# The first batch's a and b by column halves, a later place for the second weight halves, and wider, longer-lasting warm-up products

## The chip, the cores and the metric

The kernel runs on one core of one Trainium2 chip. The metric is the device time of one execution in microseconds (us); the median of several runs counts. A core has a matrix engine (TensorE, PE in the profile), VectorE (DVE), ScalarE (ACT), GpSimd (POOL) and SyncE (SP), which here does nothing but issue the DMAs.

## The reference

Attention with a decay bias, then two feed-forward stages, all float32. There are 4 batches, 8 heads, 576 positions, 64 values per head, and so 2304 tokens of 512 values.

```python
scores = q @ k.T / 8 + minimum(-(cum_i - cum_j), 0)    # masked above the diagonal
attn   = exp(scores - max);  attn /= attn.sum() + 1e-9
x = (attn @ v)                       # tokens x 512, heads side by side
a, b = x @ w1, x @ w2                # 512 -> 1024 each
h = (a * b) @ w3;  x2 = h @ w_out    # -> 1024 -> 512
h2 = x2 @ w_in                       # -> 2048
out = (h2 - tanh(h2)) @ w_out2       # -> 512
```

## The kernel before

All matrix operands after the first heads are split into a rounded high part and a low part (names ending in h and l: `xh`, `xl`, `w1h`, `w1l`, ...), and each product is three matmuls: high by high, low by high, high by low.

Nothing is issued directly. Every operation is handed to a planner (`Plan`) with its duration by a table, the buffers that it reads and writes, a priority (smaller is earlier), and, for copies and subtractions, a choice of engines. `Plan.order` lets model time run and gives each free engine the ready operation of least priority; the order that comes out is the order in which the instructions stand on each engine. On the chip each engine works through its list in that order, so an instruction that waits holds up all that stand behind it on its engine.

The start of the kernel, with which the change deals:

- **Heads.** `head` does one head: scores for tiles of queries into two PSUM banks (L568, or L570 and L571 in the split form), a DVE reduction that adds the mask, copies the scores out and takes the row maximum (L579, one for each score bank), `exp` on ACT (L585), transposes on PE (L615), the copy of their result out of PSUM on ACT (`eh`) with the low part by DVE (`el`, L322), and the product with the values (L650 in float32; L652 and L655 in the split form), whose result DVE adds up into `xf` (L662). Two heads' buffers (`e0`, `e1`, `rqk0`, `rqk1`) are in turn. Group 0 of a head is queries 0 to 319, group 1 queries 320 to 575. For batch 0 all eight heads do group 0 first, then all eight do group 1 (only the first two of this second pass in float32); batch 1 is likewise done by groups. The normalized result is split into `xh`, `xl`.
- **Weights.** `convert` loads 128 x 512 numbers of float64 (`wraw`, 512 KB), makes float32 of them with one ACT operation (L422) and four of DVE (L423, L424, L426, L428, into one of three `wt` buffers), and splits that into high (ACT or DVE) and low (POOL or DVE, L324 or L322). `w1` and `w2` are 16 such pieces: 8 for columns 0 to 511 (priority 790), 8 for columns 512 to 1023 (the second halves, priority 790 + `convq`).
- **a and b.** `products(b, half)` does, for one half of a batch's queries (288), the eight column blocks f = 0 to 7 of a and b: 12 matmuls of 288 columns each for a and for b (L710), so 24 for a block, and then a copy `asb` and a DVE product into `cst` (L718). Blocks 0 to 3 need the first weight halves only, blocks 4 to 7 the second. Their PE priority is above 1.0e6, behind every head's. The next batch's heads go on while PE works at them.
- **Warm-up products.** `filler` is a bf16 matmul on zeros. One stands at the start; and wherever PE would be idle in model time before `fu`, `Plan.order` puts as many as fit. Before the change that ends with the first matmul of `products`.

The rest of the kernel (from some 400 us) computes `wa` = w3 by w_out, x2, and the last stage; the change does not touch it.

Of the kernel before, what the change touches and what calls it, by code (L numbers as in the profile page):

```python
# [34 lines left out]
XT = [(t, min(t + 512, NT)) for t in range(0, NT, 512)]  # L35
MASKED8 = -8.0e9
NR = D + 10
PARAM = dict(dsub=1000.0, dsub0=1000.0, dcopy=1000.0, dcopy0=600.0, dother=1000.0, dother0=1000.0, spi=500.0, lay=6, lay0=4, layp=2.2e5, layf=2.95e5, gate=0, dve0=1000.0, early=100.0e3, raw0=0, rawp=-700.0, ng=3, nosb=2, cut=(1,), convq=400.0, natb=2, abk=1, wap=0.95e6, dve=1000.0, act=0.0, pool=0.0, sem=160.0, pesem=180.0, slow=1.1, convp=790.0, npre=4,
             nbias=3, keep=0.5, ff=0.0, fu=60.0e3, wlast=8, bw=370.0, ntr=3, actb=1, actn=0, spp=-80.0, ne=2, nsb=2, ncf=5, outlag=15)

LO_CLAMP = 2.0 ** -15 * 1.125
HI_CLAMP = 2.0 ** 16 * (2.0 - 2.0 ** -3 - 2.0 ** -20)
# [18 lines left out]


class Op:
    __slots__ = ("opts", "eng", "lat", "fn", "prio", "deps", "succ", "n", "ready", "start", "end", "dur", "as_", "ae", "two", "kind")


class Plan:
# [14 lines left out]
    def op(self, opts, r=(), w=(), prio=0.0, lat=0.0, two=False, kind=None):  # L82
        o = Op()
        o.kind = kind
        o.two = two
        o.opts = {e: (d, fn) for e, d, fn in opts}
        o.prio, o.lat, o.eng = prio, lat, None
        o.deps = set()
# [21 lines left out]
    filler = None  # L110

    def busy(self, a, b):
        while a < b:
# [13 lines left out]
    def order(self):  # L127
# [30 lines left out]
                push(o)  # L158
        done = []
        pair = 0.0  # L160
        while True:
            best = None
            for e in free:
# [31 lines left out]
                free[e] = t + 50.0  # L195
                continue
            if e == "PE":
                if got.prio >= 1.0e6:
                    self.fill_until = 0.0
                while self.fill_from < free[e] and free[e] + 60.0 < t < self.fill_until:  # L200
                    f = Op()
                    f.eng, f.fn, f.start, f.prio, f.lat, f.deps = e, self.filler, free[e], 9e9, 0.0, ()
                    f.dur = 60.0 * self.clock(free[e])
                    f.end = f.start + f.dur
                    self.busy(f.start, f.end)
                    done.append(f)
                    free[e] = f.end
                t = max(t, free[e])
            got.eng = e
            got.dur, got.fn = got.opts[e]  # L210
            if e == "POOL" or (e == "DVE" and got.two):
                t = max(t, pair)
# [4 lines left out]
            if e == "PE":  # L217
                self.busy(t, got.end)
            free[e] = got.end
            done.append(got)  # L220
            for x in got.succ:
                x.n -= 1
# [35 lines left out]
def tile_kernel(ctx, tc, qk, v, s, w1, w2, w3t, w_out, w_in, w_out2, out):  # L258
# [51 lines left out]
    wt_d = Buf(NF2)  # L310
    wt_d.t = dram.tile([NF2, P, 512], F32, name="wt_d")


    def dma(dst, src, nbytes, r, w, prio):
        pl.op([("SP", max(PARAM["spi"], 60.0 + nbytes / PARAM["bw"]), lambda: nc.sync.dma_start(dst(), src()))], r=r, w=w, prio=prio, lat=2000.0)
# [18 lines left out]
    def dve(fn, n, r, w, prio, fast=False, two=False, extra=0.0):  # L334
        pl.op([("DVE", c_dve(n, fast) + extra, fn)], r=r, w=w, prio=prio, two=two or fast)
# [10 lines left out]
    wu = keep.buf("wu", [P, 32])  # L346
# [12 lines left out]
    asb_r = abp.ring("asb", 2, [P, HALF])  # L359

    att = Pool("att", "right")
    msk = att.buf("msk", [P, S])
# [91 lines left out]
    def values():  # L454
        m = nc.vector.memset
        m(fix.t[:NH], 1.0)
        m(fix.t[D:D + 5], 1.0)
        for R in rqk:
            m(R.t[D:D + 32, S:], 0.0)
        m(const.t[:, 0:1], SQ_B)  # L460
        m(const.t[:, 1:2], -T2)
        m(ssum.t, 1.0)
        m(msk.t, 0.0)
# [7 lines left out]
    pl.op([("DVE", 2700.0, values)], w=[const, ssum, msk, eh, el, en, fix] + [(R, 1) for R in rqk] + e2, prio=-2900)  # L471
# [6 lines left out]
    pl.op([("POOL", 3000.0, patterns)], w=[ident, (fix, 1), msk], prio=-2500)  # L478


    def constants(i):
# [4 lines left out]
    dve(lambda: nc.vector.memset(wu.t, 0.0), 32, [], [wu], -3000, fast=True)  # L486
# [5 lines left out]
    pe(50.0, filler, [wu], [bank[7]], -3000)  # L492

    for i in range(2):
        dma(lambda i=i: rqk[i].t[D:D + 5, :S], lambda: fix.t[D:D + 5], 5 * S * 4, [(fix, 1)], [(rqk[i], 1)], -990)
# [195 lines left out]
            split(lambda: XH.t[:, c, qa:qb], (XH, ps), lambda: XL.t[:, c, qa:qb], (XL, ps), lambda: X.t[:, qa:qb], qb - qa, [X], pr + 110)  # L691


    def products(b, half):
        XH, XL = xh[b % 2], xl[b % 2]
        o = half * HALF
        for f in range(NF):
            if f % 2 == 0:
                cs = cst_r.next()
            ab = []  # L700
            for wh, wl in ((w1h, w1l), (w2h, w2l)):
                bk = ab_ring.next()

                for k0 in range(0, KC, PARAM["abk"]):
                    ks = range(k0, min(k0 + PARAM["abk"], KC))

                    def mm(bk=bk, wh=wh, wl=wl, f=f, ks=ks):
                        for k in ks:
                            for j, (w_, x_) in enumerate(((wh, XH), (wh, XL), (wl, XH))):
                                nc.tensor.matmul(bk.t[:, :HALF], w_.t[:, k, f * P:(f + 1) * P], x_.t[:, k, o:o + HALF],  # L710
                                                 start=k == 0 and j == 0, stop=k == KC - 1 and j == 2)
                    parts = [k * 2 + f // 4 for k in ks]
                    xs = [2 * k + g for k in ks for g in range(1 + half)]
                    pe(3 * len(ks) * c_pe(HALF), mm, [(XH, xs), (XL, xs), (wh, parts), (wl, parts)], [bk], 1.0e6 + ((b * 2 + half) * NF + f))
# [27 lines left out]
    for b in range(B):  # L742
# [7 lines left out]
        else:  # L750
# [175 lines left out]
```

## Time and profile before

| | before |
|---|---|
| runs | 996.61, 997.66, 1001.73 us; median 997.66 |
| the profiled execution | 1001.11 us, of which the span from first to last instruction is 999.3 us |
| PE, DVE, ACT, POOL busy | 97%, 72%, 60%, 39% of the span |
| TensorE's mean granted clock | 0.976 of full |

A share of busy time is a mean over stages. The "granted clock" is the share of TensorE's full rate that the chip let through: 1.00 is 2.4 GHz, 0.50 is 1.2 GHz. PE's busy time is modelled, and at half clock everything on it takes about twice as long, so a busy PE may do half the work; the number of matmuls in a stretch (x..) says more. The trace may lack a few matmul records.

### The profile page before, as it was taken

To read this page: it belongs to the slowest core of one execution; us is meant where nothing else is said; L and a number is where in the kernel's file an instruction comes from. 1 tells how busy PE (TensorE), PEld (TensorE's weight loads), DVE (VectorE), ACT (ScalarE), POOL (GpSimd) and SP (SyncE) were. 2 spreads that over 40 slices of the span, in tenths; PEclk is the share of its full clock that TensorE was granted. 3 is DMA by queue.
4 is the path that set the end of the run, shared out by engine and by line. 5 is a ranking of instruction groups with operands and counts; after the bars stand their busy time and mean duration, and the time that the engine had idled before them with its cause. 6 is when DMAs were issued, how large, how long until landed. Compare 5 with 4: busy or idle time off the path is not lost.

```text
span 999.3 us, 16720 instructions
## 1 busy us (share of the span) xinstructions
PE 967.4 (97%) x5715; PEld 839.3 (84%) x5715; DVE 720.6 (72%) x1453; ACT 602.8 (60%) x1378; POOL 393.8 (39%) x338
## 2 busy tenths in 40 slices
PE   7988799999998999999999999999999999999998
PEld 6557599999998999888988898878888888888897
DVE  7579878887898876998688879895544545545455
ACT  4575577878887874444354538566545555555565
POOL 2245646643654633433254647442222222222221
PEclk7799699999999999999999999999999999999999
DMA  5476246565555413546769865103002100200010
GB/s 160 134 210 204 91 123 191 179 193 176 159 158 153 131 48 110 183 166 231 248 234 334 275 216 201 42 22 127 1 1 85 43 0 1 85 1 1 1 43 22
DMA packets 70093, 124.47 MB, mean 125 GB/s; under 512 B 6780, under 2 KB 39172, under 8 KB 70008
## 3 DMA queue, kind: packets, MB, share of 16 engines
q1 hardware_dynamic: 70008, 123.41, 38.7%
q8 instruction: 45, 0.74, 0.3%
q14 instruction: 40, 0.33, 0.1%
HBM read 93.34 MB, written 25.99 MB: 119 GB/s over the span
## 4 chain that ended last, share of the span: by engine, by line
PE 85%; DVE 6%; DMA 3%; issue 2%; ACT 2%; POOL 1%; SPq 0%; DVEq 0%; ACTq 0%; POOLq 0%
PE bank L851 19%; PE bank L710 16%; PE bank L874 6%; PE bank L873 6%; PE bank L872 6%; PE bank L615 5%; PE bank L815 3%; PE bank L814 3%; PE bank L813 3%; PE bank L570 2%; PE bank L652 2%; PE bank L655 2%; PE bank L571 2%; PE bank L568 2%; PE bank L775 1%
## 5 line engine op out<-in xcount | busy, mean ns | idle before, releaser
L324 POOL TENSOR_TENSOR gl<-pg,gh 128x512 fp32r<-128x512 f32 (+1 forms) x78 | 98.6, 1264 | 261.0 <-ACT gh L318 248.0
L851 PE MATMUL bank<-x2b,wih 128*128 128x512 f32 (+1 forms) x640 | 183.0, 371 | 0.0
L862 DVE TENSOR_TENSOR pg<-bank,u 128x512 f32<-128x512 f32 (+1 forms) x80 | 50.8, 635 | 142.7 <-ACT th L861 140.6
L851 PEld LDWEIGHTS bank<-x2b,wih 128*128 128x128 f32 x640 | 116.6, 188 | 22.5
L851 PE MATMUL bank<-x2b,wil 128*128 128x512 f32 (+1 forms) x320 | 118.7, 371 | 0.0
L874 PE MATMUL bank<-voh,gl 128*128 128x512 f32 x288 | 112.8, 392 | 0.5 <-POOL gl L324 0.4
L872 PE MATMUL bank<-voh,gh 128*128 128x512 f32 x288 | 112.7, 391 | 0.2 <-ACT gh L318 0.2
L873 PE MATMUL bank<-vol,gh 128*128 128x512 f32 x288 | 112.8, 392 | 0.0
L318 ACT ACTIVATE gh<-pg 128x512 fp32r<-128x512 f32 (+1 forms) x80 | 47.1, 589 | 87.3 <-DVE pg L866 86.6
L585 ACT ACTIVATE e<-e,nmx 64x64 f32<-64x64 f32 (+4 forms) x160 | 88.7, 556 | 12.0 <-DVE nmx L579 11.5
L615 PE MATMUL bank<-ident,e 128*128 128x128 f32 (+1 forms) x480 | 82.8, 283 | 5.1 <-DVE el L322 3.1
L859 ACT ACTIVATE u<-bank 128x512 f32<-128x512 f32 (+1 forms) x80 | 44.3, 553 | 70.9 <-PE bank L851 67.0
L422 ACT ACTIVATE wt<-wraw 128x512 f32<-128x512 f32 x72 | 47.9, 671 | 63.9 <-DMA wraw<-w3t 14.6
L710 PE MATMUL bank<-xh,w1h 128*128 128x288 f32 x256 | 81.8, 319 | 3.7 <-ACT asb L318 2.1
L579 DVE CUSTOM_DVE_ANT_0 e<-bank,msk 64x64 f32<-64x64 f32 (+4 forms) x160 | 64.5, 417 | 27.9 <-PE bank L568 14.4
L710 PE MATMUL bank<-xh,w2h 128*128 128x288 f32 x256 | 81.1, 317 | 2.9 <-DVE cst L718 2.4
L710 PE MATMUL bank<-xh,w2l 128*128 128x288 f32 x256 | 76.2, 298 | 3.0 <-POOL w2l L324 3.0
L710 PE MATMUL bank<-xh,w1l 128*128 128x288 f32 x256 | 76.6, 299 | 2.1 <-POOL w1l L324 2.1
L322 DVE TENSOR_TENSOR el<-bank,eh 128x512 fp32r<-128x512 f32 (+1 forms) x162 | 73.2, 473 | 5.0 <-ACT eh L318 4.3
L710 PE MATMUL bank<-xl,w1h 128*128 128x288 f32 x256 | 76.0, 297 | 0.0
L710 PE MATMUL bank<-xl,w2h 128*128 128x288 f32 x256 | 75.7, 296 | 0.0
L866 DVE COPY_PREDICATED pg<-mk,th 128x512 f32<-128x512 uint32 (+1 forms) x80 | 62.8, 785 | 12.5 <-ACT mk L864 4.6
(137 smaller groups left out, 2624.5 us busy)
## 6 DMA issues: line engine op xcount, KB each, us to landing
rqk<-qk SPq DMA_DIRECT2D x30, 576.0 KB
wraw<-w_out SPq DMA_DIRECT2D x24, 512.0 KB
c_d<-cst SPq DMA_DIRECT2D x32, 288.0 KB
wraw<-w SPq DMA_DIRECT2D x16, 512.0 KB
wraw<-w3t SPq DMA_DIRECT2D x16, 512.0 KB
cf<-c_d SPq DMA_DIRECT2D x32, 256.0 KB
wraw<-w_in SPq DMA_DIRECT2D x16, 512.0 KB
x_d<-x2s SPq DMA_DIRECT2D x16, 512.0 KB
```

Source lines behind the costliest of these rows:

```text
L322: o = [("DVE", c_dve(n), lambda: nc.vector.tensor_tensor(dst(), a(), b().bitcast(F32), op=ALU.subtract))]
L324: o.append(("POOL", c_pool2(n), lambda: nc.gpsimd.tensor_tensor(dst(), a(), b().bitcast(F32), op=ALU.subtract)))
L579: nc.vector.tensor_tensor_reduce(e.t[:nq, EOFF[t] + k0:EOFF[t] + k1], bk.t[:nq, :k1 - k0], bi.t[:nq, bo + k0:bo + k1], -0.125, 3.0e38 if f ...
L585: act(lambda: nc.scalar.activation(et(), et(), AF.Exp, bias=nmx.t[:nq, i, tm:tm + 1], scale=-1.0, accum_out=ssum.t[:nq, pj, t, i:i + 1]), ...
L615: nc.tensor.transpose(bk.t[:rows, n * P:(n + 1) * P], e.t[:, EOFF[t] + c * P:EOFF[t] + c * P + rows], ident.t)
L710: nc.tensor.matmul(bk.t[:, :HALF], w_.t[:, k, f * P:(f + 1) * P], x_.t[:, k, o:o + HALF], start=k == 0 and j == 0, stop=k == KC - 1 and j ...
L851: nc.tensor.matmul(bk.t[:, :w], w_.t[:, k, a], X2.t[:, i, k, :w], start=k == 0 and n == 0, stop=k == KC - 1 and n == 2)
L862: dve(lambda u=u, pg=pg, hp=hp, c_=c_: nc.vector.tensor_tensor(c_(pg), hp(), c_(u), op=ALU.mult), w, [bk, u], [pg], pr)
L866: dve(lambda pg=pg, mk=mk, th=th, c_=c_: nc.vector.copy_predicated(c_(pg), c_(mk).bitcast(U32), c_(th)), w, [mk, th], [pg], pr, two=True)
L872: nc.tensor.matmul(bank[n].t, gh.t[:, a], voh[f].t, start=f == 0, stop=False)
L873: nc.tensor.matmul(bank[n].t, gh.t[:, a], vol[f].t, start=False, stop=False)
L874: nc.tensor.matmul(bank[n].t, gl.t[:, a], voh[f].t, start=False, stop=f == NF2 - 1)
```

## The change

Four edits. `products` takes the blocks that it is to do; for batch 0 the order is blocks 0 to 3 for both halves of the queries, then blocks 4 to 7 for both, and the priorities count up in that order. `convq` goes from 400 to 1200: the second weight halves' conversions have priority 1990 in place of 1190, which is behind all heads of batch 0 (priorities up to some 1600) and among those of batch 1. The warm-up product is 128 x 128 in place of 64 x 64, reads zeros in the first 64 columns of the mask `msk`, and writes bank 2, the bank of the product with the values, in place of bank 7. And it may be put into PE's idle time up to 150 us of model time (60 before), also behind the first matmul of `products`, but not between a write and the last read of bank 2.

```diff
-... convq=400.0 ... fu=60.0e3 ...
+... byf=(0,) ... convq=1200.0 ... fu=150.0e3 ...
...
-                if got.prio >= 1.0e6:
-                    self.fill_until = 0.0
-                while self.fill_from < free[e] and free[e] + 60.0 < t < self.fill_until:
+                while self.fill_from < free[e] and free[e] + 110.0 < t < self.fill_until and not unread and free[e] >= read:
...
-                    f.dur = 60.0 * self.clock(free[e])
+                    f.dur = 107.0 * self.clock(free[e])
...
     def filler():
-        x = wu.t.bitcast(BF16)
-        nc.tensor.matmul(bank[7].t[:D, :D], x[:, :D], x[:, :D], start=True, stop=True)
+        x = msk.t[:, :D].bitcast(BF16)
+        nc.tensor.matmul(bank[2].t[:, :P], x, x, start=True, stop=True)
...
-    def products(b, half):
+    def products(b, half, fs):
...
-        for f in range(NF):
+        for f in fs:
+            pos = 1.0e6 + n_prod[0]
+            n_prod[0] += 1
...
-        for half in range(2):
-            products(b, half)
+        for fs in (range(4), range(4, NF)) if b in PARAM["byf"] else (range(NF),):
+            for half in range(2):
+                products(b, half, fs)
```

What this does to the lists of instructions is seen at three places. All lines of the changed kernel are 9 to 13 higher, and buffers have other numbers behind the underscore.

On DVE the two lists are the same up to the sum `xf1` of the third head in batch 0's second pass (the fourth head's three reductions on `e1` are done by then). Before, the conversions of the second weight halves follow it:

```order
160 L662 TENSOR_TENSOR xf1_126<-bank2_60,pvt_124 64x256
161 L428 SCALAR_TENSOR_TENSOR wt0_83<-wraw1_82,wt0_83 128x512
162 L718 TENSOR_TENSOR cst1_132<-bank7_65,asb0_133 128x288
...
170 L424 TENSOR_SCALAR wt2_89<-wt2_89 128x512
171 L423 TENSOR_SCALAR wt0_83<-wt0_83 128x512
172 L426 SCALAR_TENSOR_TENSOR wt2_89<-wraw2_88,wt2_89 128x512
173 L322 TENSOR_TENSOR el_123<-bank5_63,eh_122 64x128
174 L423 TENSOR_SCALAR wt1_84<-wt1_84 128x512
175 L424 TENSOR_SCALAR wt0_83<-wt0_83 128x512
176 L428 SCALAR_TENSOR_TENSOR wt2_89<-wraw2_88,wt2_89 128x512
```

The fifth head's first reduction comes 31 rows behind `xf1`. In the changed kernel it is the next row, and the sixth head's follow:

```order
160 L671 TENSOR_TENSOR xf1_125<-bank2_60,pvt_123 64x256
161 L588 ISA e0_115,nmx_117<-bank0_58,msk_103 128x448
162 L588 ISA nmx_117 128x1
163 L731 TENSOR_TENSOR cst1_131<-bank7_65,asb0_132 128x288
164 L332 TENSOR_TENSOR el_122<-bank3_61,eh_121 128x4x128
165 L588 ISA e0_115,nmx_117<-bank1_59,msk_103 128x288
...
173 L437 SCALAR_TENSOR_TENSOR wt0_82<-wraw1_81,wt0_82 128x512
174 L731 TENSOR_TENSOR cst1_131<-bank7_65,asb1_133 128x288
175 L332 TENSOR_TENSOR el_122<-bank5_63,eh_121 64x128
176 L588 ISA e1_116,nmx_117<-bank1_59,msk_103 128x448
```

The seven pieces of the second weight halves that are unfinished at that row (one lacks only its last operation) have moved from one block into the gaps of the next eight heads; the last of the 16 conversions stands, as before, ahead of the sum for batch 1's fourth head.

On PE, in the seventh head of that second pass, the products that stood between the heads' matmuls are gone, and warm-up products (`msk`) stand there. Before (`xh`, `xl` by w1, w2 are the products):

```order
843 L570 MATMUL bank_59<-kh_112,qs_111 128x288
844 L571 MATMUL bank_59<-kl_113,q_114 128x288
845 L710 MATMUL bank_64<-xh_90,w1h 128x288
846 L710 MATMUL bank_64<-xl_92,w1h 128x288
847 L710 MATMUL bank_64<-xh_90,w1l 128x288
848 L570 MATMUL bank_58<-kh_112,qs_111 128x288
849 L571 MATMUL bank_58<-kl_113,q_114 128x288
850 L710 MATMUL bank_65<-xh_90,w2h 128x288
```

And of the changed kernel:

```order
594 L579 MATMUL bank_58<-kh_111,qs_110 128x448
595 L580 MATMUL bank_58<-kl_112,q_113 128x448
596 L579 MATMUL bank_59<-kh_111,qs_110 128x288
597 L580 MATMUL bank_59<-kl_112,q_113 128x288
598 L499 LDWEIGHTS msk
599 L499 MATMUL bank_60<-msk 128x128
600 L499 LDWEIGHTS msk
601 L499 MATMUL bank_60<-msk 128x128
```

Counted in the two lists, there stand ahead of the eighth head's product with the values in that pass 201 matmuls of `products` before and 114 now, ahead of that of batch 1's fourth head in its first group 261 and 180, of batch 1's ninth such product 375 and 342, and from the 34th behind batch 0 on (786 ahead) the two are level again. Warm-up products: 283 before, 179 of them at the start; 218 now, 100 at the start, 47 up to the first matmul of `products`, and 71 behind it.

On SP's queue only the last three loads of the second weight halves change place among the heads' loads; before, two of them stood together:

```order
97 L315 DMA wraw3_108<-w1 128x1024
98 L315 DMA wraw2_88<-w2 128x1024
99 L315 DMA rv1_109<-v 128x320
100 L315 DMA kl0_113<-kb_d_68 10x576
101 L315 DMA q20_114<-qs0_111 64x256
```

Now the seventh head's `kl0` is ten rows further up and ahead of all three, of which the first stands here:

```order
90 L325 DMA kl0_112<-kb_d_68 10x576
91 L325 DMA q21_796<-qs1_793 64x256
92 L325 DMA r_d_69<-rinv1_120 4x128
93 L325 DMA rqk1_106<-qk 128x1152
94 L325 DMA xr_126<-r_d_69 64x2x128
95 L325 DMA q20_113<-qs0_110 64x256
96 L325 DMA wraw1_81<-w2 128x1024
```

The other two are now at rows 103 and 115.

## Rows read from the trace of the kernel before

**Rows 1.** The page: the chain that ended last, by engine.
```profile
PE 85%; DVE 6%; DMA 3%; issue 2%; ACT 2%; POOL 1%; SPq 0%; DVEq 0%; ACTq 0%; POOLq 0%
```

**Rows 2.** Stretches: length, each engine's busy time, granted clock, DMA share, GB/s.
```profile
15.00:35.00 20.00, 19.22 (x96) 12.01 (x96) 8.62 (x33) 9.17 (x32) 3.01 (x2) 0.50 0.38 110
40.00:60.00 20.00, 19.84 (x120) 12.43 (x120) 15.72 (x42) 14.35 (x49) 9.55 (x10) 1.00 0.64 192
75.00:95.00 20.00, 18.34 (x131) 16.69 (x129) 17.90 (x33) 12.88 (x32) 12.28 (x11) 1.00 0.65 207
88.00:156.00 68.00, 57.09 (x387) 51.90 (x386) 55.95 (x137) 45.71 (x127) 38.50 (x40) 0.85 0.44 133
...
94.00:116.00 22.00, 12.74 (x42) 9.49 (x43) 19.12 (x32) 10.34 (x21) 13.67 (x11) 0.54 0.35 108
...
116.00:142.00 26.00, 25.49 (x203) 24.66 (x201) 20.88 (x61) 20.08 (x58) 11.83 (x14) 1.00 0.40 115
...
300.00:320.00 20.00, 17.21 (x126) 16.24 (x125) 17.69 (x51) 15.12 (x44) 10.39 (x9) 0.91 0.52 149
```

**Rows 3.** Whom PE waited for, 87 to 116 us: total, times, longest.
```profile
PE bank L710 <- POOL w2l L324: 3.0, 2, 2.4
PE bank L710 <- POOL w1l L324: 2.1, 3, 0.7
PE bank L710 <- DVE cst L718: 1.8, 1, 1.8
PE bank L710 <- ACT w1h L318: 1.6, 2, 0.9
PE bank L570 <- DVE nmx L579: 1.1, 1, 1.1
PE bank L710 <- ACT w2h L318: 0.5, 1, 0.5
```

**Rows 4.** DVE in order of time, 88 to 112 us: start, duration, instruction, idle before.
```profile
88.36 0.42 DVE L662 TENSOR_TENSOR xf<-bank,pvt 64x256 f32<-64x256 f32 x1 [0.36 <-ACT pvt L318]
88.70 0.67 DVE L428 SCALAR_TENSOR_TENSOR wt<-wraw,wt 128x512 uint32<-128x512 uint32 x1
...
92.82 1.89 DVE L428 SCALAR_TENSOR_TENSOR wt<-wraw,wt 128x512 uint32<-128x512 uint32 x1
...
95.93 1.49 DVE L423 TENSOR_SCALAR wt<-wt 128x512 f32<-128x512 f32 x1
97.34 0.68 DVE L426 SCALAR_TENSOR_TENSOR wt<-wraw,wt 128x512 uint32<-128x512 uint32 x1
...
98.14 0.41 DVE L423 TENSOR_SCALAR wt<-wt 128x512 f32<-128x512 f32 x1
...
105.02 1.64 DVE L426 SCALAR_TENSOR_TENSOR wt<-wraw,wt 128x512 uint32<-128x512 uint32 x1
106.87 1.20 DVE L423 TENSOR_SCALAR wt<-wt 128x512 f32<-128x512 f32 x1 [0.22 <-ACT wt L422]
...
109.76 1.65 DVE L428 SCALAR_TENSOR_TENSOR wt<-wraw,wt 128x512 uint32<-128x512 uint32 x1
111.44 0.42 DVE L662 TENSOR_TENSOR xf<-bank,pvt 64x256 f32<-64x256 f32 x1
111.89 0.62 DVE L579 CUSTOM_DVE_ANT_0 e<-bank,msk 128x448 f32<-128x448 f32 x1
```

**Rows 5.** PE in order of time: products with the values, heads five, eight and batch 1's fourth.
```profile
119.30 0.69 PE L652 MATMUL bank<-eh,vs 128*128 128x256 f32 x5
...
138.26 0.69 PE L652 MATMUL bank<-eh,vs 128*128 128x256 f32 x5
...
155.68 0.50 PE L652 MATMUL bank<-eh,vs 128*128 128x320 f32 x3
```

**Rows 6.** PE waits, 298 to 318 us, in order of time (idle before an instruction).
```profile
304.16 0.21 PE L570 MATMUL bank<-kh,qs 128*64 128x64 f32 x1 [0.37 <-DVE nmx L579]
309.18 0.30 PE L615 MATMUL bank<-ident,e 128*64 128x128 f32 x1 [1.81 <-DVE el L322]
```

**Rows 7.** POOL in order of time, around the slow DVE operations at 105 and 110 us.
```profile
104.66 1.45 POOL L324 TENSOR_TENSOR w1l<-wt,w1h 128x512 fp32r<-128x512 f32 x1 [0.47 <-ACT w1h L318]
...
109.41 1.45 POOL L324 TENSOR_TENSOR w1l<-wt,w1h 128x512 fp32r<-128x512 f32 x1 [1.62 <-ACT w1h L318]
```

**Rows 8.** PE in order of time, 1 to 15 us, and its first-pass products with the values.
```profile
1.02 8.19 PE L490 MATMUL bank<-wu 128*64 128x64 bf16 x179 [1.02 <-DVE wu L486]
13.05 0.94 PE L568 MATMUL bank<-rqk 69*64 69x64 f32 x4 [3.84 <-DMA rqk<-rel]
13.92 0.96 PE L490 MATMUL bank<-wu 128*64 128x64 bf16 x14
...
25.90 2.61 PE L650 MATMUL bank<-en,rv 128*64 128x320 f32 x6
...
40.20 1.40 PE L650 MATMUL bank<-en,rv 128*64 128x320 f32 x6
...
57.29 1.40 PE L650 MATMUL bank<-en,rv 128*64 128x320 f32 x6
```

**Rows 9.** PE in order of time, its last warm-up products from 6.26 us.
```profile
6.26 2.94 PE L490 MATMUL bank<-wu 128*64 128x64 bf16 x81
```

More of the change, by code (lines that the diff above doesn't have):

```diff
@@ L37 @@
 NR = D + 10
-PARAM = dict(dsub=1000.0, dsub0=1000.0, dcopy=1000.0, dcopy0=600.0, dother=1000.0, dother0=1000.0, spi=500.0, lay=6, lay0=4, layp=2.2e5, layf=2.95e5, gate=0, dve0=1000.0, early=100.0e3, raw0=0, rawp=-700.0, ng=3, nosb=2, cut=(1,), convq=400.0, natb=2, abk=1, wap=0.95e6, dve=1000.0, act=0.0, pool=0.0, sem=160.0, pesem=180.0, slow=1.1, convp=790.0, npre=4,
-             nbias=3, keep=0.5, ff=0.0, fu=60.0e3, wlast=8, bw=370.0, ntr=3, actb=1, actn=0, spp=-80.0, ne=2, nsb=2, ncf=5, outlag=15)
+PARAM = dict(byf=(0,), dsub=1000.0, dsub0=1000.0, dcopy=1000.0, dcopy0=600.0, dother=1000.0, dother0=1000.0, spi=500.0, lay=6, lay0=4, layp=2.2e5, layf=2.95e5, gate=0, dve0=1000.0, early=100.0e3, raw0=0, rawp=-700.0, ng=3, nosb=2, cut=(1,), convq=1200.0, natb=2, abk=1, wap=0.95e6, dve=1000.0, act=0.0, pool=0.0, sem=160.0, pesem=180.0, slow=1.1, convp=790.0, npre=4,
+             nbias=3, keep=0.5, ff=0.0, fu=150.0e3, wlast=8, bw=370.0, ntr=3, actb=1, actn=0, spp=-80.0, ne=2, nsb=2, ncf=5, outlag=15)
 LO_CLAMP = 2.0 ** -15 * 1.125
@@ L63 @@
 class Op:
-    __slots__ = ("opts", "eng", "lat", "fn", "prio", "deps", "succ", "n", "ready", "start", "end", "dur", "as_", "ae", "two", "kind")
+    __slots__ = ("opts", "eng", "lat", "fn", "prio", "deps", "succ", "n", "ready", "start", "end", "dur", "as_", "ae", "two", "kind", "bank")
 class Plan:
@@ L87, in op @@
         o.prio, o.lat, o.eng = prio, lat, None
+        o.bank = None
+        for x, items in (("r", r), ("w", w)):
+            if any((it[0] if isinstance(it, tuple) else it) is self.fill_bank for it in items):
+                o.bank = x
         o.deps = set()
@@ L109 @@
     fill_until, fill_from = 0.0, 0.0
-    filler = None
+    filler = fill_bank = None
     def busy(self, a, b):
@@ L160, in order @@
         pair = 0.0
+        unread, read = set(), 0.0
         while True:
@@ L209, in order @@
             got.eng = e
+            if got.bank == "w":
+                unread = set(x for x in got.succ if x.bank == "r")
+            unread.discard(got)
             got.dur, got.fn = got.opts[e]
@@ L219, in order @@
             free[e] = got.end
+            if got.bank == "r":
+                read = got.end + self.SEM[e] + 100.0
             done.append(got)
@@ L311, in tile_kernel @@
     wt_d.t = dram.tile([NF2, P, 512], F32, name="wt_d")
+    pl.fill_bank = bank[2]
     def dma(dst, src, nbytes, r, w, prio):
@@ L345, in tile_kernel @@
     rel = nat.buf("rel", [3 * NH, 3 * S], n=6)
-    wu = keep.buf("wu", [P, 32])
     xp = Pool("xp", "right")
@@ L361, in tile_kernel @@
     att = Pool("att", "right")
-    msk = att.buf("msk", [P, S])
+    msk = att.buf("msk", [P, S], n=2)
     fix = att.buf("fix", [P, S], n=2)
@@ L462, in values @@
         m(ssum.t, 1.0)
-        m(msk.t, 0.0)
+        m(msk.t[:, D:], 0.0)
         for e in e2:
@@ L470, in values @@
             m(x.t[D:, o + 1024:].bitcast(F32), 0.0)
-    pl.op([("DVE", 2700.0, values)], w=[const, ssum, msk, eh, el, en, fix] + [(R, 1) for R in rqk] + e2, prio=-2900)
+    pl.op([("DVE", 2700.0, values)], w=[const, ssum, (msk, 1), eh, el, en, fix] + [(R, 1) for R in rqk] + e2, prio=-2900)
     def patterns():
@@ L477, in patterns @@
         nc.gpsimd.affine_select(msk.t[:, 448:], msk.t[:, 448:], [[-1, P]], ALU.is_ge, MASKED8, 0, 1)
-    pl.op([("POOL", 3000.0, patterns)], w=[ident, (fix, 1), msk], prio=-2500)
+    pl.op([("POOL", 3000.0, patterns)], w=[ident, (fix, 1), (msk, 1)], prio=-2500)
     def constants(i):
@@ L483, in constants @@
             dma(lambda a=a: q2[i].t[a:a + 5].bitcast(F32), lambda: fix.t[D:D + 5], 5 * S * 4, [(fix, 1)], [(q2[i], 1)], 400)
-    dve(lambda: nc.vector.memset(wu.t, 0.0), 32, [], [wu], -3000, fast=True)
+    dve(lambda: nc.vector.memset(msk.t[:, :D], 0.0), D, [], [(msk, 0)], -3000, fast=True)
     def filler():
-        x = wu.t.bitcast(BF16)
-        nc.tensor.matmul(bank[7].t[:D, :D], x[:, :D], x[:, :D], start=True, stop=True)
+        x = msk.t[:, :D].bitcast(BF16)
+        nc.tensor.matmul(bank[2].t[:, :P], x, x, start=True, stop=True)
     pl.filler, pl.fill_from, pl.fill_until = filler, PARAM["ff"], PARAM["fu"]
-    pe(50.0, filler, [wu], [bank[7]], -3000)
+    pe(50.0, filler, [(msk, 0)], [bank[2]], -3000)
     for i in range(2):
@@ L713, in products @@
                     xs = [2 * k + g for k in ks for g in range(1 + half)]
-                    pe(3 * len(ks) * c_pe(HALF), mm, [(XH, xs), (XL, xs), (wh, parts), (wl, parts)], [bk], 1.0e6 + ((b * 2 + half) * NF + f))
+                    pe(3 * len(ks) * c_pe(HALF), mm, [(XH, xs), (XL, xs), (wh, parts), (wl, parts)], [bk], pos)
                 ab.append(bk)
```

1 line of the change is left out of this document (added).

## The prediction

> **What bounds the kernel now.** I read the chain of waits first: 85% of it is PE [rows 1], so what PE does not get done at some point has to be made up by nobody else. Then the stretches, looking at the matmul counts and the clock and not at PE's busy time [rows 2]. From 116 to 142 us PE does 203 matmuls in 26 us, 7.8 a microsecond, at a granted clock of 1.00. From 94 to 116 us it does 42 in 22 us at 0.54. At 7.8 a microsecond 42 matmuls are 5.4 us of work, so some 16.6 us of PE are lost there. The list of waits names the cause [rows 3]: 9.0 us of waits of L710, nearly all for pieces of w1 and w2 that ACT or POOL was still splitting, and the low clock on top. PE had run out of blocks 0 to 3 and stood before block 4.
>
> DVE in that stretch is the third thing to read [rows 4]. The sum for the third head ends at 88.8 us; the fifth head's first reduction starts at 111.89 us. In between DVE does 19.12 of 22 us [rows 2] of mostly conversions. So the heads stood still for 23 us while PE, which could have worked for them, waited for the weights.
>
> Is PE alone the bound behind 116 us? Not quite. At 300 to 320 us PE does 126 matmuls in 20 us where 156 would fit, at a clock of 0.91, and waits for the heads' DVE results [rows 2, 6]: its stock of products is used up, and what counts there is how far the heads are. The heads' pace and PE's lost time are thus two bounds that meet near 310 us; a gain has to be one by both.
>
> **The change part by part. The move on DVE.** It adds and removes no operation there. I compare one state in both kernels: all 16 conversions done and the product with the values of batch 1's fourth head done, 155.68 us before [rows 5]. From 88 to 156 us DVE is busy 55.95 us [rows 2], and that work is the same but for the order. What can change is how densely DVE does it. Before, it was 0.87 dense in the block of conversions (19.12 / 22) and 0.80 while PE was full (20.88 / 26) [rows 2]; there the heads' short chains from PE to DVE to ACT and back queued behind products on PE. In the changed kernel PE has little besides heads in this stretch, for 87 of the products that stood ahead of the eighth head are gone. The nearest row for such a mix of heads and conversions with PE not full is 75 to 95 us: 17.90 / 20 = 0.895 [rows 2]. At 0.895 the 55.95 us take 62.5 us in place of 68: 5.5 us gained. The bounds are 0.80 (69.9 us, 1.9 us lost) and 1.00 (12 us gained).
>
> A second thing lies in the 55.95 us. Five conversion operations in the block are far longer than their like: 1.89, 1.64 and 1.65 us against 0.67 or 0.68, 1.49 and 1.20 against 0.41 [rows 4]. Their excess is 1.22 + 0.96 + 0.97 + 1.08 + 0.79 = 5.0 us, and beside the ones at 105.02 and 109.76 us POOL was in a 1.45 us subtraction [rows 7]. Spread among the heads' DVE operations, fewer conversions meet a POOL subtraction; I take half of the excess as saved, between none and all. Then (55.95 - 2.5) / 0.895 = 59.7 us, 8.3 us gained. Between 5.5 and 8.3 I take **7 us**.
>
> The Trainium skill (GPSIMD Engine Reference, the table at its head) says that GpSimd shares its SBUF interfaces with VectorE, in contention with DVE instructions in a two-port mode or with two SBUF inputs. The trace agrees: the long ones are of just these kinds. By that rule POOL's subtractions for the heads could stretch the moved conversions as much as POOL's own conversions did, and the sum would be the lower 5.5; by the rows alone it lies anywhere from 5.5 to 11 (50.95 / 0.895 = 56.9).
>
> **Does PE allow it?** 387 matmuls were done from 88 to 156 us [rows 2]. In the changed list 81 fewer products stand ahead of the same state. The other 306 are 39 us at 7.8 a microsecond, in 61 us. So PE has 22 us to spare and follows the heads. It then has 81 matmuls, 10 us, of stock in hand, and the lists show this stock shrink to 33 (4.2 us) at batch 1's ninth product with the values and to nothing near 310 us, where before some 30 matmuls (3.8 us) could not be done for want of stock. So the heads' 7 us hold to that point, and behind it the lists are level and PE is the bound in both.
>
> **The warm-up products behind the first product.** 71 of them. 81 narrow ones took 2.94 us [rows 9], 36 ns each; twice as wide, an estimate of 73 ns, 5.2 us in all. They lie in stretches where PE has the 22 us to spare; I cost them at nothing. If that cover is gone, up to 5 us. Each also waits until ACT and DVE have read bank 2, and the heads' matmuls queue behind it; the planner puts it behind that read in its own time, and I have no row for it: bounds nothing and 2 us, I take nothing.
>
> **The start.** The 100 wide warm-up products have 1.12 times the columns of 179 narrow ones, which took 8.19 us [rows 8]: an estimate of 9.2 us, to 10.2 us. The first scores still wait for the landing of `rqk` at 13.05 us [rows 8], whose place on SP is unchanged. PE idled 3.84 us ahead of it and then ran at a clock of 0.50 from 15 to 35 us [rows 2]; now it idles some 2.9 us. If the clock falls all the same, nothing changes. If it came back a head earlier, that head would take 4.3 us in place of 7.2: from 25.90 to 40.20 us two heads pass at low clock, 7.2 us each, from 40.20 to 57.29 four, 4.3 each [rows 8]. So nothing to 6 us gained (two heads); nearest to the row is nothing.
>
> **The loads.** The last three weight loads stand up to 17 rows later on SP, and their conversions are later by more. I cost them at nothing.
>
> **Sum.** -7 + 0 + 0 + 0 = -7 us. The profiled execution took 1001.11 us, 1.8 us more than its span and 3.5 us more than the median of 997.66. Its changed counterpart would take 994; the median 990.7, say **991 us**.
>
> **Rivals.** *The clock also comes back sooner at the start.* For it: wider products and a shorter idle time. Against it: still near 3 us of idle. 4 us more: 986 us.
>
> *No change.* The heads gain no density, because two heads' buffers and two score banks hold them and not PE; for it speaks the 0.80 of 116 to 142 us, though PE was full there. Or block 4 is late once more: its weights now end just ahead of the state I compare, and products in PE's list wait for them with heads queued behind; the same 9.0 us of waits [rows 3] would use up the 7. Time 995 to 1000, say 998 us.
>
> *Slower, by the clock.* Between 94 and 135 us PE now has heads with gaps in place of products. The clock was 0.50 while PE did first-pass heads with gaps [rows 2, 8], and 1.00 in the same work from 40 us. If PE sits at 1.2 GHz for part of this, each head costs 7.2 - 4.3 = 2.9 us more. Up to 7 / 2.9 = 2.4 heads there is still no loss; with five, 14.5 - 7 = 7.5 us lost, 1005 us. Against it: the warm-up products, 71 of them, stand in just these gaps.
>
> **How the numbers follow.** Forecast 0.45, the sooner clock 0.15, no change 0.25, the slow clock 0.15. A measurement of this kernel tells about 0.5% (5 us) from no change. The first two are faster by more: 0.60; the third is the same: 0.25; the fourth slower: 0.15. The forecast's own range is 986 to 995. The range for 8 in 10 leaves out most of the slow clock (0.12) and the far end of the two gains at once (-11 and -6, 0.05): 982 to 1003.
>
> **What would show it.** In the changed profile: the fifth head's first reduction near 89 us, not 111.89, and, if four heads take the 26.4 us that they took from there to 138.26, the eighth's product with the values near 115; batch 1's fourth near 149, not 155.68; DVE about 0.9 dense from 88 to 149; some 300 matmuls there, with a clock of 1.00; block 4's weights near 146 us without waits of L723 for them; no gap near 310 us bigger than before. At the start, the low clock from about 14 to 37 us as before. I am wrong if the eighth head's product comes later than 121 us or the clock falls between 94 and 140 (slower cases), or if the heads are early and time is lost again between 150 and 310 us: then the heads are not the bound that I take them for.

## The result, and the profile after

The changed kernel takes 986.1 us (median of 5 runs, 983.64 to 987.05) against 1000.04 us for the kernel before (median of 5, 996.61 to 1001.73); the ratio is 0.9841, with a 95% interval of 0.9815 to 0.9867. That is 16 us faster by the ratio and 14 by the two medians, where 7 were forecast; 986.1 lies in the stated range. A second set of runs of the same kernel gave 0.9870 (0.9849 to 0.9890), 13 us. The profiled executions took 1001.11 and 984.61 us, spans 999.3 and 982.9 us.

On the page, the chain of waits still ends mostly on PE:

```profile
PE 82%; DVE 7%; DMA 5%; issue 2%; ACT 2%; POOL 1%; SPq 0%; DVEq 0%; POOLq 0%; ACTq 0%
```

The stretches of the changed kernel, columns as in [rows 2] (PE, PEld for its weight loads, DVE, ACT, POOL, then the granted clock). The first two are the start; 81 to 137 us is the counterpart of 88 to 156, from the third head's sum to the end of the last conversion:

```profile
15.00:35.00 20.00, 19.97 (x113) 13.30 (x111) 15.33 (x53) 14.59 (x51) 4.42 (x3) 0.84 0.56 166
40.00:60.00 20.00, 17.52 (x103) 11.75 (x102) 16.16 (x39) 15.15 (x42) 10.05 (x11) 1.00 0.66 201
...
81.00:137.00 56.00, 48.71 (x374) 45.11 (x374) 53.47 (x128) 43.53 (x123) 39.51 (x41) 0.94 0.54 160
...
94.00:116.00 22.00, 17.60 (x133) 16.13 (x132) 20.66 (x56) 19.18 (x56) 14.04 (x16) 0.84 0.60 174
116.00:142.00 26.00, 24.44 (x192) 23.33 (x191) 23.93 (x59) 18.21 (x56) 19.11 (x21) 1.00 0.33 92
106.70:113.50 6.80, 6.08 (x28) 5.98 (x29) 6.25 (x17) 5.10 (x16) 4.81 (x5) 0.50 0.46 128
300.00:320.00 20.00, 19.09 (x153) 18.27 (x152) 16.67 (x50) 16.47 (x47) 10.05 (x9) 1.00 0.69 213
```

The stretch that took 68 us takes 56, and DVE is 53.47 / 56 = 0.955 dense in it. From 300 to 320 us PE does 153 matmuls where it did 126: its stock of products no longer runs out. The half clock between the heads has not gone, but lasts 6.8 us (106.7 to 113.5) in place of some 20.

PE in order of time, products with the values of the third, fifth and eighth head and of batch 1's fourth:

```profile
78.80 0.69 PE L661 MATMUL bank<-eh,vs 128*128 128x256 f32 x5
...
94.28 0.70 PE L661 MATMUL bank<-eh,vs 128*128 128x256 f32 x5
...
114.90 0.78 PE L661 MATMUL bank<-eh,vs 128*128 128x256 f32 x5
...
132.68 0.48 PE L661 MATMUL bank<-eh,vs 128*128 128x320 f32 x3
```

The last three stood at 119.30, 138.26 and 155.68 us [rows 5]. So the heads are 23 us ahead at batch 1's fourth, and the end of the kernel comes 16 us earlier: the other 7 us are work that PE still has to do, since fewer products stand ahead of that point.

DVE at the place where the lists part (start, duration, instruction, idle before); the fifth head's reduction follows the third head's sum at once, 81.58 us in place of 111.89 [rows 4]:

```profile
81.24 0.42 DVE L671 TENSOR_TENSOR xf<-bank,pvt 64x256 f32<-64x256 f32 x1 [0.34 <-ACT pvt L328]
81.58 0.61 DVE L588 CUSTOM_DVE_ANT_0 e<-bank,msk 128x448 f32<-128x448 f32 x1
```

PE's waits from 81 to 149 us are now mostly for DVE's results (reductions, `el`) and not for weights; L723 is the line of the matmuls for a and b:

```profile
PE bank L579 <- DVE nmx L588: 2.9, 4, 1.1
PE bank L603 <- DVE el L332: 2.8, 1, 2.8
...
PE bank L723 <- DVE cst L731: 0.2, 1, 0.2
```

The start, PE in order of time. The wide warm-up products end at 8.3 us, earlier than the 10.2 that I had worked out, and the idle time ahead of the first scores is longer than before, 4.69 us:

```profile
1.05 7.27 PE L499 MATMUL bank<-msk 128*128 128x128 bf16 x100 [1.05 <-DVE msk L495]
13.02 1.38 PE L577 MATMUL bank<-rqk 69*64 69x64 f32 x4 [4.69 <-DMA rqk<-rel]
```

All the same the half clock ended near 21 us and not near 37, and the third head's product with the values stands at 78.80, not at 85.89 us: of the 16.5 us between the two profiled executions 7.1 are there before the heads' lists part.

### The profile page after: what moved, and what is told of

Its sections match the earlier page's. It is cut to its first block, busy times and chain, and to the rows that moved or that the text cites. A ratio compares the mean times of both kernels' runs of the same rounds, so it can differ in the third digit from the quotient of the medians.

```text
span 982.9 us, 16588 instructions
## 1 busy us (share of the span) xinstructions
PE 955.8 (97%) x5650; PEld 835.4 (85%) x5650; DVE 721.6 (73%) x1449; ACT 603.7 (61%) x1379; POOL 400.1 (41%) x341
## 4 chain that ended last, share of the span: by engine, by line
PE 82%; DVE 7%; DMA 5%; issue 2%; ACT 2%; POOL 1%; SPq 0%; DVEq 0%; POOLq 0%; ACTq 0%
PE bank L865 19%; PE bank L723 16%; PE bank L888 6%; PE bank L886 6%; PE bank L887 6%; PE bank L624 4%; PE bank L828 3%; PE bank L827 3%; PE bank L829 3%; PE bank L661 2%; PE bank L664 2%; PE bank L579 2%; PE bank L580 2%; DMA xr<-r_d 2%; PE bank L791 1%
## 5 line engine op out<-in xcount | busy, mean ns | idle before, releaser
L624 PE MATMUL bank<-ident,e 128*128 128x128 f32 (+1 forms) x480 | 80.8, 277 | 3.4 <-ACT e L594 1.4
L723 PE MATMUL bank<-xh,w2h 128*128 128x288 f32 x256 | 80.6, 315 | 1.4 <-DVE cst L731 1.4
L723 PE MATMUL bank<-xh,w1h 128*128 128x288 f32 x256 | 81.3, 318 | 0.6 <-ACT asb L328 0.3
L723 PE MATMUL bank<-xl,w2h 128*128 128x288 f32 x256 | 75.7, 296 | 0.0
L723 PE MATMUL bank<-xh,w1l 128*128 128x288 f32 x256 | 75.7, 296 | 0.0
L723 PE MATMUL bank<-xl,w1h 128*128 128x288 f32 x256 | 75.6, 295 | 0.0
L723 PE MATMUL bank<-xh,w2l 128*128 128x288 f32 x256 | 75.5, 295 | 0.0
L332 DVE TENSOR_TENSOR el<-bank,eh 128x512 fp32r<-128x512 f32 (+2 forms) x162 | 73.5, 474 | 2.5 <-ACT eh L328 2.0
```

The source lines that it names most:

```text
L332: o = [("DVE", c_dve(n), lambda: nc.vector.tensor_tensor(dst(), a(), b().bitcast(F32), op=ALU.subtract))]
L624: nc.tensor.transpose(bk.t[:rows, n * P:(n + 1) * P], e.t[:, EOFF[t] + c * P:EOFF[t] + c * P + rows], ident.t)
```

## The experiments

Two theories stood at first. **Two gains**: the wide warm-up products shorten the half clock at the start (6 to 7 us), and the heads' order on DVE gives the rest. **Order alone**: the start came out better by chance. Where nothing else is said, the lists are those of the kernel that a variant starts from, instruction by instruction, but for the warm-up products.

**The kernel before with wide warm-up products.**

```diff
-        nc.tensor.matmul(bank[7].t[:D, :D], x[:, :D], x[:, :D], start=True, stop=True)
+        nc.tensor.matmul(bank[7].t[:, :P], x, x, start=True, stop=True)
```

> The kernel before, with each of its 283 warm-up products 128 x 128 wide (zeros from the mask, bank 7); every list is otherwise that of before. Theory 'two gains' (the start gains 6 to 7 us by an earlier full clock that the width brings, the heads' order gains the rest): the half clock that lasted from 14 to 37 us ends near 21 us, the products with the values of the first pass come 6 to 7 us earlier, and the time is 6 to 7 us below before, ratio 0.993 to 0.994. Rival 'order alone' (the start came out better by chance of the clock's phase): clock and time as before, ratio 0.998 to 1.002.

Measured: 993.54 us, ratio 0.9931 (0.9901 to 0.9960). In its stretches at the start (columns as above) there is no half clock at all in the profiled execution, and DVE gets through half as much again as before:

```profile
13.00:21.00 8.00, 5.98 (x66) 4.80 (x67) 6.35 (x21) 5.44 (x17) 1.75 (x1) 1.00 0.41 124
21.00:29.00 8.00, 8.00 (x56) 5.35 (x56) 6.45 (x20) 5.08 (x19) 1.27 (x1) 1.00 0.63 172
29.00:37.00 8.00, 8.00 (x60) 5.50 (x59) 6.34 (x21) 6.09 (x23) 1.40 (x1) 1.00 0.78 211
```

The gain is of the size that "two gains" asked for. The profiled execution, 988.70 us, was the fastest of the seven (mean clock 0.991; the others 0.985 to 0.991), so some of the others may have had half clock here. And the 179 wide products also filled PE's idle time up to 12.6 us, so width and filling are not told apart by this run.

**The changed kernel with narrow ones.** At each of the 218 places:

```diff
-        nc.tensor.matmul(bank[2].t[:, :P], x, x, start=True, stop=True)
+        nc.tensor.matmul(bank[2].t[:D, :D], x[:, :D], x[:, :D], start=True, stop=True)
```

> The changed kernel, with each of its 218 warm-up products 64 x 64 at the places where the wide ones stand; every list is otherwise that of the changed kernel. Theory 'two gains': the half clock lasts to near 37 us, and 6 to 7 us of the gain are lost, ratio 0.990 to 0.992 of before. Rival 'order alone': 0.984 as the changed kernel.

Measured: 990.89 us, ratio 0.9906 (0.9875 to 0.9937). The half clock lasted to some 29 us in the profiled execution, not to 37. The ratio is where "two gains" had it, with its interval (up from 0.9875) little above the 0.984 of that theory's rival; but the half clock that was to explain it did not come to 37 us. Against the second set of the changed kernel (0.9870) the loss is 4 us and the intervals overlap.

**Without the late warm-up products**, and **with neither these nor the width.** The function that issues them:

```diff
+        n_fill[0] += 1
+        if n_fill[0] > 147:
+            return
```

> The changed kernel without the 71 warm-up products behind the first matmul of products; the 147 ahead of it stay wide, every list is otherwise that of the changed kernel. Theory 'two gains': the heads' stretch from 81 to 137 us is as dense on DVE (0.95), the half clock there lasts longer than the 6.8 us of the changed kernel, and the time is 0 to 3 us above it, ratio 0.984 to 0.988. Rival 'the late products carry it' (without them PE goes to half clock for 20 us or more among the heads and each loses some 2.9 us): 7 us or more above it, ratio 0.991 or higher.

Measured: 985.84 us, 0.9852 (0.9823 to 0.9880). The 71 late ones are worth nothing that can be measured, in cost or in gain. This kernel has the wide products at the start, and still its half clock lasted to 29 us, as with the narrow ones of narrow_after. From 21 to 29 us, this kernel and then narrow_after:

```profile
21.00:29.00 8.00, 8.00 (x29) 4.71 (x27) 3.49 (x13) 3.65 (x13) 1.26 (x1) 0.50 0.43 126
21.00:29.00 8.00, 8.00 (x29) 4.48 (x27) 3.51 (x13) 3.81 (x15) 1.26 (x1) 0.50 0.42 124
```

> The changed kernel with narrow 64 x 64 warm-up products and none behind the first matmul of products: what is left of the change is the order of the blocks and of the second weight halves. Theory 'two gains': 6 to 10 us above the changed kernel, ratio 0.990 to 0.994, half clock to near 37 us and again among the heads. Rival 'order alone': 0.984 to 0.986.

Measured: 987.55 us, 0.9869 (0.9838 to 0.9901), between the ranges of the two theories. So what is left of the change gives 13 us, between 10 and 16. That is not all the heads' order, for fewer warm-up products stand at the start than before (100 for 179), and in the profiled execution the third head's product comes at 82.66 us, 3.2 us earlier than before. The difference to the kernel with the width, 2 us, is not told from nothing in this pair. In the kernel before, the wide products gave 7 us; in the changed kernel the width is worth from nothing to some 6.

**One order edit without the other.** Here the planner makes its lists anew. First `convq` back at 400:

> The changed kernel with the second weight halves' priority as before (790 + 400 in place of 790 + 1200); the planner makes its lists anew. Theory 'the heads go first': the conversions stand in one block again, the fifth head's first reduction comes some 20 us later than in the changed kernel, and the part of the gain that is the heads' (7 to 9 us) is lost while the start's 6 to 7 us stay: ratio 0.990 to 0.994. Rival 'the block order does it' (blocks 0 to 3 of the other query half fill PE whatever the conversions' place): 0.984 to 0.987.

Measured: 1005.12 us, 1.0022 (1.0002 to 1.0042). The whole gain is gone, though the third head's product with the values still stands at 79.2 us, 6.7 us ahead of the kernel before: from there to the end this kernel is 9 us slower than before. Both theories missed. PE in order of time, its longest wait (in brackets):

```profile
105.73 0.61 PE L579 MATMUL bank<-kh,qs 128*128 128x288 f32 x1 [13.94 <-DVE nmx L588]
```

And its stretches, columns as above:

```profile
94.00:116.00 22.00, 9.31 (x63) 8.62 (x64) 15.50 (x38) 11.38 (x27) 13.63 (x11) 0.69 0.27 85
116.00:142.00 26.00, 22.34 (x183) 19.56 (x182) 20.74 (x69) 22.69 (x76) 16.41 (x23) 1.00 0.46 126
140.00:160.00 20.00, 18.00 (x135) 17.40 (x134) 14.23 (x46) 14.05 (x48) 12.10 (x17) 0.93 0.54 156
```

DVE converts in one block again; PE waits 13.94 us for a reduction. When the second weight halves are there, near 105 us, nothing uses them: in PE's list blocks 0 to 3 of the other query half stand ahead of block 4, and they need all heads of the second pass. The first such block's product by DVE starts at 137.2 us, where the changed kernel has it at 122.2 and the one before did block 4 at 117.8.

Then the old block order with the late conversions (`byf=()`):

> The changed kernel with batch 0's blocks 0 to 7 for one query half after the other, as before, and the second weight halves still late; the planner makes its lists anew. Theory 'the heads go first': DVE's work is as dense, but PE stands longer without products, since block 4 of the first query half comes ahead of block 0 of the second: 1 to 5 us above the changed kernel, ratio 0.985 to 0.989. Rival 'the block order does it': 0.991 or higher.

Measured: 1001.15 us, 0.9992 (0.9968 to 1.0017). The first theory missed again; the rival's bound was met, but its reason, that the block order does it, is contradicted by convq400. The stretches:

```profile
94.00:116.00 22.00, 17.26 (x114) 15.13 (x112) 20.63 (x46) 15.10 (x44) 13.55 (x14) 0.77 0.44 125
116.00:142.00 26.00, 17.68 (x108) 15.32 (x109) 23.42 (x58) 19.05 (x59) 17.05 (x19) 0.81 0.35 98
```

Now it is the mirror image: the heads go first and are early, DVE is 0.9 dense, but block 4 of the first query half stands next in PE's list and its weights come at 139 us. From 116 to 142 us PE does 108 matmuls (17 of them warm-up products), where the changed kernel does 192 (4). Here too the third head's product is early, at 78.09 us, and the rest takes 10 us longer than before. The two edits are one: what is converted late must be wanted late.

**Filling the idle time at the start.** This became the rival of the width: wide_before had done both.

```diff
-        nc.tensor.matmul(...)
+        for _ in range(70 if n_fill[0] == 1 else 1):
+            nc.tensor.matmul(...)
```

> The changed kernel with 69 more wide warm-up products at the very start, so that PE's idle time of 4.7 us ahead of the first scores (released at 13.0 us) is nearly filled; every list is otherwise that of the changed kernel. If the half clock from 11.1 to 21.3 us comes from that idle time, the clock stays full through the first heads and the time is 2 to 4 us lower, ratio 0.980 to 0.982. If it comes from the heads' own gaps, the clock falls all the same a little later and the time is that of the changed kernel, 0.984; if the products run past 13 us, it is up to 2 us above it.

Measured: 981.37 us, 0.9805 (0.9762 to 0.9849). Its half clock at the start lasted 3.4 us, from 17.3 to 20.7; the idle time ahead of the first scores was 1.21 us. The stretches:

```profile
13.00:21.00 8.00, 6.10 (x49) 4.89 (x47) 6.00 (x16) 4.24 (x14) 1.75 (x1) 0.79 0.47 137
21.00:29.00 8.00, 8.00 (x50) 5.13 (x48) 7.04 (x24) 6.08 (x22) 1.27 (x1) 1.00 0.59 169
```

The next four ran as one set. The changed kernel once more:

> The changed kernel once more, unchanged, beside the three that follow: 0.984 of before by any theory.

Measured: 987.91 us, 0.9870 (0.9849 to 0.9890). Its profiled execution had the half clock from 12.6 to 29.7 us, where the first one's ended at 21: the same list does not always get the same clock. The stretches:

```profile
13.00:21.00 8.00, 5.60 (x35) 4.23 (x34) 5.66 (x16) 3.74 (x12) 1.75 (x1) 0.50 0.48 135
21.00:29.00 8.00, 8.00 (x29) 5.14 (x29) 3.00 (x11) 3.41 (x14) 1.27 (x1) 0.50 0.39 115
29.00:37.00 8.00, 8.00 (x43) 4.64 (x41) 6.88 (x23) 5.99 (x22) 1.41 (x1) 0.96 0.43 116
```

The kernel before, its start lengthened by narrow products (`range(96 ...)` in the same loop):

> The kernel before with 95 more of its narrow 64 x 64 warm-up products at the very start (274 in place of 179, to end near 12.5 us in place of 9.2); every list is otherwise that of before. Theory 'the idle time' (what the wide products did for the kernel before was to fill PE's idle time ahead of the first scores): the half clock behind 13 us is gone or far shorter than the 23.9 us of before, and the time is 5 to 7 us lower, ratio 0.993 to 0.995. Rival 'the width': half clock to near 37 us as before, ratio 0.998 to 1.002.

Measured: 1002.01 us, 0.9984 (0.9955 to 1.0013). In the profiled execution (1002.82 us) PE's warm-up products reach to 11.8 us, 1.94 us of idle time are left, and the half clock is as long as ever (14.3 to 38.2 us):

```profile
13.00:21.00 8.00, 6.40 (x55) 4.32 (x56) 5.69 (x16) 3.22 (x10) 1.75 (x1) 0.58 0.49 137
21.00:29.00 8.00, 8.00 (x39) 5.05 (x37) 3.00 (x11) 3.32 (x13) 1.26 (x1) 0.50 0.39 117
29.00:37.00 8.00, 8.00 (x27) 4.48 (x27) 3.80 (x13) 3.82 (x13) 0.00 (x0) 0.50 0.20 52
```

By the profiled execution "the idle time" falls for narrow products. But four of the twelve executions took 992.31 to 996.97 us, at a mean clock of 0.987 or 0.988; the other eight took 1001.0 to 1005.37 at 0.974 to 0.981, and none of the 23 of the kernel before beside them was above 0.983. From 0.976 to 0.988 is some 24 us less at half clock (an estimate: 0.012 of 1000 us, twice), about as long as the half clock at the start. None of these four was profiled, but it looks as if narrow products, too, take that half clock away in some executions. And the narrow filling left 1.94 us idle, where wide_before left none (first scores at 12.56 us):

```profile
13.76 0.96 PE L572 MATMUL bank<-rqk 69*64 69x64 f32 x4 [1.94 <-DMA rqk<-rel]
12.56 0.85 PE L567 MATMUL bank<-rqk 69*64 69x64 f32 x4
```

So this pair does not settle width against filling.

> The changed kernel with 40 more wide warm-up products at the very start (140; with 69 more they ran to 13.5 us, past the landing that releases the first scores). Theory 'the idle time': the idle time shrinks from 4.7 us to some 2 us, the half clock behind it is shorter than the changed kernel's 10.2 us, and the time is 2 to 4 us below that of the changed kernel in the same set, ratio 0.980 to 0.982. Rival 'the width has done it all': within 1 us of the changed kernel.

Measured: 984.32 us, 0.9839 (0.9819 to 0.9860), 3.6 us below the changed kernel of the same set; the idle time was 2.40 us and the half clock 3.4 us long. The intervals overlap a little, so the 3.6 us are likely, not certain. With the wide products, filling the idle time does seem to help.

**The place of the second weight halves.**

```diff
-convq=1200.0
+convq=1500.0
```

> The changed kernel with 69 more wide warm-up products at the start and the second weight halves later still (790 + 1500). Theory 'block 4 must be ready when blocks 0 to 3 of both query halves are done' (convq400 and no_byf each lost the whole gain, PE standing without products to 137 and 142 us): later conversions make PE wait for block 4, some 3 to 8 us more than with 1200, ratio 0.984 to 0.989. Rival 'heads first, the later the better': 0.980 or lower.

Measured: 998.24 us, 0.9979 (0.9959 to 1.0000): some 17 us worse than with 1200 and the same start, in the direction of the theory of block 4, which had asked for 3 to 8. From 140 to 160 us PE runs dry, at a clock of 0.83:

```profile
140.00:160.00 20.00, 15.42 (x100) 14.09 (x99) 14.38 (x40) 12.79 (x38) 14.32 (x15) 0.83 0.50 151
```

In its list of waits (total, times, longest) block 4's weights stand first; L727 is the product here:

```profile
PE bank L727 <- POOL w1l L334: 3.1, 1, 3.1
```

> The changed kernel with 69 more wide warm-up products at the start and the second weight halves somewhat earlier (790 + 1000 in place of 790 + 1200). With 400 the gain is lost since PE stands without products while DVE converts, with 1500 since PE stands before block 4. Theory 'just in time': 1000 lies between, the conversions meet the heads of early batch 1, and the time is within 5 us of the kernel with 1200 and the same start, ratio 0.978 to 0.985. Rival 'earlier costs at once' (each conversion ahead of a head delays blocks 0 to 3 of the second query half): ratio 0.988 or higher.

Measured: 984.75 us, 0.9847 (0.9820 to 0.9874), within 5 us of the 981.37 with 1200 and the same start; the intervals overlap, so 1000 and 1200 are not told apart, while 1500 and 400 are worse. The 169 wide products left only 0.97 us idle in the profiled execution, and still the half clock lasted from 17.5 to 27.7 us, three times as long as in long_start with the same start. The lowest time of all versions is that of the changed kernel with the longer wide start, 0.9805; its interval (0.9762 to 0.9849) overlaps with that of the changed kernel.

**Start and rest told apart.** The third head's product with the values stands close to where the heads' order changes, behind the start. The columns are its start and the time from there to the end of the span, in us, one profiled execution of each kernel:

| kernels | third head's product | from there to the end |
|---|---|---|
| order of before: before, wide_before, narrow_long_before | 85.89, 77.08, 86.82 | 913.4, 909.8, 914.3 |
| both order edits, wide: changed kernel, after_again, no_late_fill | 78.80, 81.18, 81.88 | 904.1, 905.0, 903.8 |
| both order edits, narrow: narrow_after, order_only | 80.83, 82.66 | 905.1, 903.9 |
| both order edits, longer wide start: long_start, long_start_140 | 76.61, 77.89 | 902.0, 904.2 |
| one order edit: convq400, no_byf | 79.21, 78.09 | 922.1, 923.6 |

The lines for before, order_only, convq400 and no_byf:

```profile
85.89 0.70 PE L652 MATMUL bank<-eh,vs 128*128 128x256 f32 x5
82.66 0.70 PE L666 MATMUL bank<-eh,vs 128*128 128x256 f32 x5
79.21 0.69 PE L661 MATMUL bank<-eh,vs 128*128 128x256 f32 x5
78.09 0.70 PE L661 MATMUL bank<-eh,vs 128*128 128x256 f32 x5
```

The two order edits together make the rest some 8 to 9 us shorter on average (910 to 914 against 902 to 905), each alone makes it 8 to 14 us longer, and the start accounts for what is left of the gain. With `convq` at 1500 and 1000 it is 916.0 and 906.8.

## Why the prediction was right, and where it was too small

**The bound.** Right. PE's loss between 94 and 116 us came from the heads' standstill on DVE. The fifth head's reduction follows the third head's sum at once, PE does 133 matmuls from 94 to 116 us in place of 42 (27 of the 133 are warm-up products, and 44 of the 374 from 81 to 137 us), and the weights are no longer waited for. Of the 9.0 us of waits [rows 3] 1.8 were for DVE's `cst` and not for weights; that changes nothing here.

**The move on DVE: right in kind, too small.** I wrote 0.895 for the density, from the nearest row; it is 0.955. By the same sum 55.95 us at 0.955 would be 58.6 us, 9.4 gained, against 12 in the stretch itself, where 53.47 us of DVE work sufficed (fewer blocks of products fall in it). Why it is denser is not shown. That PE has less to do is not enough: from 116 to 142 us PE is busy 24.44 of 26 us and DVE is 23.93 / 26 = 0.92 dense, where it was 0.80 before with PE busy 25.49; conversions spread among the heads, which fill DVE's gaps, would fit. The traces put the order at some 8 to 9 us behind the third head's product (904 against 912.5 on average), where I had 7. That 7 came so near is luck in part: the density gave more than I took, and the excess that I took as saved was not saved.

**The excess of long conversions: wrong.** I took half of 5.0 us as saved. In the changed kernel they are longer: 3.02 against 0.41 us at 132.25, 1.83 against 0.41 at 108.48, 1.58 against 0.67 at 86.45; these three alone have 4.9 us of excess. DVE in order of time:

```profile
86.45 1.58 DVE L437 SCALAR_TENSOR_TENSOR wt<-wraw,wt 128x512 uint32<-128x512 uint32 x1
...
108.48 1.83 DVE L433 TENSOR_SCALAR wt<-wt 128x512 uint32<-128x512 uint32 x1
...
132.25 3.02 DVE L432 TENSOR_SCALAR wt<-wt 128x512 f32<-128x512 f32 x1
```

And POOL around the second of these:

```profile
107.41 1.36 POOL L334 TENSOR_TENSOR kl<-rqk,kh 64x320 fp32r<-64x320 f32 x1
108.74 1.28 POOL L334 TENSOR_TENSOR w1l<-wt,w1h 128x512 fp32r<-128x512 f32 x1
```

POOL is at the heads' `kl` and then at `w1l`. The rule cited from the Trainium skill (GPSIMD Engine Reference, the table at its head) spoke for just this, and the trace agrees with it better than with the value that I took.

**Does PE allow it?** Right: 374 matmuls in 56 us, no wait of note for products, and the stock of them lasts over 310 us. The heads' 23 us did not all become time, since PE became the bound behind them, as both bounds had to allow.

**The warm-up products behind the first product.** Costed at nothing; nothing was measured (0.9852 without them).

**The start: the step that failed.** I took nothing of a range of nothing to 6 us, because the idle time ahead of the first scores would stay. It did stay, 4.69 us. But the half clock ended sooner, and the five profiled executions of the changed order with 100 products at the start have 3.2 to 7.1 us there (third head's product at 78.80 to 82.66 us in place of 85.89). The width is not all of it: the two with narrow products are among them, with 3.2 and 5.1 us. In the kernel before the wide products gave 7 us (4 to 10); in the changed kernel narrow_after lies 4 to 6 us above it, order_only 2 above no_late_fill. So the rival "the clock also comes back sooner" was the case, on top of the forecast, and its number, 986 us, is the one that was measured; what brought the clock back is open.

**The slow clock** between the heads came, for 6.8 us, and cost the seventh and eighth head little: their products with the values are 7.8 and 6.4 us behind the one before, the fifth's and sixth's 5.3 and 6.5. By my own sign (wrong if the clock falls between 94 and 140 us) this spoke for the slower cases, but 6.8 us of it were too short for that. Another sign was met by luck: the eighth head's product stands at 114.90 us, where I had 115, but the heads began 7 us earlier than I took and needed 33 us to that place in place of 26.4. Batch 1's fourth, at 132.68 us, came far ahead of the 149 that I had.

**The rival "no change"** has the time that each order edit gives alone, but only since the early start makes up for a loss: convq400 loses by the conversions' block, no_byf by block 4 coming too late. I had named the second mechanism, with the 9.0 us of waits as its price; no_byf loses 10 us behind the third head's product.

What stays open: how much of the start's gain each execution gets, since the half clock of the same list ended at 21 us once and at 30 us once; whether it is the width, the filled time or the number of the warm-up products that shortens it; and whether the wide products work by their place ahead of the first scores or between the heads. No run had the one without the other.

## What to carry to other kernels

When one engine prepares operands for two consumers, look for the stretch in which one consumer's work stands still behind the preparation for the other, and move the preparation behind the work that is ready; but move the consumer's order with it, for either alone may lose more than both gain. Price such a move from more than one row: the one that looked nearest gave a density of 0.895, and 0.955 came. When a change acts at two places, find an instruction between them and compare the time ahead of it and behind it; the totals alone mixed the start with the order here. And do not read the cause of a clock from one execution: the same list got its full clock back at 21 us in one and at 30 us in the other.

## What the runs showed of the hardware

In one profiled execution each: filling PE's time up to 11.8 us with 64 x 64 bf16 products left the granted clock at 0.50 from 21 to 37 us (narrow_long_before; four of its twelve executions had a mean clock higher by some 0.01); 128 x 128 products up to 12.6 us had it at 1.00 from 13 to 37 us (wide_before). With wide products at the start of the changed kernel the half clock ended at 21.3, 29.7 and 29.0 us in three executions (changed kernel, after_again, no_late_fill). One hundred wide products took 7.27 us in one execution and 8.01 in another, 179 narrow ones 8.19. A 128 x 512 clamp on DVE, 0.41 us by itself, took 3.02 us in the worst place, from 132.25 us, with POOL in two subtractions of 1.27 and 1.30 us from 131.90 to 134.43 us.
